# Attention with pooled keys, then a mixture of adapters: the order of operations at the start and at the end of the kernel is written out by hand

## Chip, core and metric

The kernel runs on one core of a Trainium2 chip. The metric is the device time of one execution in microseconds. Engines: PE (TensorE, matmuls and transposes), DVE (VectorE), ACT (ScalarE), POOL (GpSimd), and SP, which only issues DMAs here. Each engine takes its instructions strictly in the order in which they stand in its queue.

## What is computed

`q` is 4 x 12288 x 128, `kv` is 4 x 384 x 32 x 128, all fp32.

```python
kv_pool = kv.reshape(B, H//4, 4, W//4, 4, C).mean(axis=(2, 4))    # 768 keys per batch
k = v = kv_pool.reshape(B, -1, C) @ w_sr
a = softmax(q @ k.T / sqrt(C))
x = (a @ v).reshape(B * N, C)                                     # 49152 rows
logits = x @ w_gate                                               # 8 experts, the best 2 used
delta = sum over the two: softmax weight * (x @ A[e]) @ B[e]      # rank 16
return x + delta
```

## The kernel before

The 49152 rows are cut into 96 chunks of 512 rows, 24 to a batch (`NB = 24`). Four chunks share one load of q (`GC = 4`). Keys come in J = 6 blocks of 128, handled as three pairs r = 0, 1, 2. For a chunk k the steps are the following (line numbers of the kernel before; all matmuls go through line 68):

- `scores(k, r)` (238): two matmuls of 128x512 into an `sg` tile of PSUM (two tiles, `ps_s`), then the exp on ACT into `em` (246).
- `attend(k, s)` for four quarters s (248): six matmuls of 128x137 each from `em` and `vx` into `acc`, of which there is one tile (`ps_a`).
- `normalize(k)` (256): on DVE a reciprocal and a product, from `acc` to `xn`. `xn` holds the 128 outputs and the 8 logits. The next chunk's attend can't write `acc` before it.
- `top(k)` (276): four MAX8 on DVE. `route` (285): comparisons on POOL (for chunks 0 and 1 on DVE). `gates` (310): a tanh on ACT and two products on POOL. Chunks are routed in pairs up to slot 71 and singly in the last batch.
- `transposes(kx, kh, engine)` (319): transposes x of one chunk and hg of an older one on PE into one PSUM tile `tt_ps`, and copies both to SBUF (`tts`) in one copy on DVE or ACT.
- `down(k)` (342), `gate(k)` (347), `up(k)` (356), `finish(k)` (361): x @ A to `h_ps`, times the gate weights on DVE (`hg`), hg @ B to `d_ps`, plus x on DVE (`osb`), and the output DMA from SP.

The PSUM tiles of q's transposes, key preparation, `tt_ps`, `h_ps` and `d_ps` share two banks (`ps_m`, tag `mb`). `osb` has six tiles.

The keys of batch 0 are prepared at the start: kv comes in 24 DMAs of 256 KB (98), DVE adds rows (`pair_step`, 175), PE transposes and sums them to `kpT`, multiplies with w_sr to `kfT` (`keys`, `keys2`) and to `vx` (`values`). For later batches POOL adds (`pool_step`, 163) while the chunks of the batch before run; nine small steps on PE and DVE follow (`rest`). q of groups 0 and 1 is loaded as fp32 and transposed on PE (`turn_q`, 107); later groups are cast to bf16 by a DMA issued from POOL (`cast_q`, 77) and transposed by a DMA from SP (`load_qT`, 82). Before each cast POOL copies one column of the qT of the group before, which makes it wait for that.

The order is that of a Python program with `keep` (program order per engine). A prologue (372 to 400) computes the scores of chunks 0 to 3 while the keys of batch 0 arrive. Then one loop (420 to 498) has a slot for each k from 4 to 95. In the plain slot, k of 9 and more:

```python
scores(k, 0); gates of an older group; normalize(k-2)
transposes(k-6, k-7, DVE); scores(k, 1); up(k-8); finish(k-8)
attend(k-1, 0); top(k-2); route (every other slot); scores(k, 2)
down(k-6); gate(k-6); a step of key preparation; attend(k-1, 1..3)
```

The dictionary `att` puts two attends into slots 6, 7 and 8, and `enter` lets two chunks instead of one enter the adapters in slots 73, 74 and 76, so that in the end the lag from chunk to adapter is shorter; their second transposes are copied by ACT. After the loop a written-out end (503 to 657) handles the adapters of chunks 91 to 95: `carry` copies d_ps to SBUF on ACT, `add_there` adds x on POOL, for two chunks; the last chunk's routing runs on DVE; the last two chunks are handled in halves.

Of the kernel before, what the change touches and what calls it, by code (L numbers as in the profile page):

```python
# [20 lines left out]
def kernel(  # L21
# [85 lines left out]
    def turn_q(g, m, engine):  # L107
        if m == 0:
            qT[g] = qpool.tile([P, GT], BF16, tag="qT", name="qT")
        ps = mtile([P, S, P], name="qT_ps")  # L110
        for i in range(S):
            mm(ps[:, i], q_f[g][:, m * S + i], id_f, is_transpose=True,
               start=(i == 0), stop=(i == S - 1))
        o = qT[g][:, m * T:(m + 1) * T].rearrange("p (s t) -> p s t", s=S)
        if engine is nc.scalar:
            keep(nc.scalar.copy(o, ps))
        else:
            keep(nc.vector.tensor_copy(o, ps))
# [39 lines left out]
    def prepare(b, adder):  # L158
# [28 lines left out]
        def keys(h):  # L187
            if h == 0:
                st["kpT"] = prep.tile([P, J, P], FP32, tag="kpT", name="kpT")
                kfT[b] = per_b.tile([P, J, P], BF16, tag="kfT", name="kfT")  # L190
            kpT = st["kpT"]
            ps = mtile([P, 2, P], name="kpT_ps")
# [4 lines left out]
            for n, (r, i, c) in enumerate(parts):  # L197
                mm(ps[:, i], kvr[b, h][:, r, i, c * C:(c + 1) * C], id_f, is_transpose=True,
                   start=(n == 0), stop=(n == len(parts) - 1))
            keep(nc.vector.tensor_scalar(kpT[:, 2 * h:2 * h + 2], ps, 1.0 / 16.0, None,  # L200
# [27 lines left out]
        for h in range(3):  # L228
            for f in (keys, keys2, values) if adder is nc.vector else (keys, values, turn):
                rest.append(lambda h=h, f=f: f(h))  # L230
# [7 lines left out]
    def scores(k, r):  # L238
        b = k // NB
        if r == 0:  # L240
# [7 lines left out]
    def attend(k, s):  # L248
        b = k // NB
        if s == 0:  # L250
# [5 lines left out]
    def normalize(k):  # L256
        ri = rpool.tile([P, S], FP32, tag="rinv", name="rinv")
        keep(nc.vector.reciprocal(ri, acc[k][:, :, VC]))  # L258
        k0, m = first[k], k - first[k]
        if m == 0:  # L260
            xg[k0] = xpool.tile([P, GC, S, VC], FP32, tag="xn", name="xn")
        x = xg[k0][:, m]
# [13 lines left out]
    def top(k):  # L276
        k0, m = first[k], k - first[k]
        if m == 0:
# [4 lines left out]
    later = []  # L283

    def route(k0):
        n = size[k0] * S
        eng = nc.gpsimd if k0 > 1 else nc.vector
        lg = xg[k0].rearrange("p m s c -> p (m s) c")[:, 0:n, C:VC]
# [72 lines left out]
    def finish(k):  # L361
# [5 lines left out]
        for d in (em, acc, xn, xT, hgT, hp, hg, dp):  # L367
            d.pop(k, None)

    LA = 4  # L370

    for m in range(GC):
        turn_q(0, m, nc.scalar)
    sums, rest = prepare(0, nc.vector)
    for h in range(3):
        for item in sums[h]:
            item()
        rest[3 * h]()
        if h > 0:
            scores(2, h - 1)  # L380
        rest[3 * h + 1]()
        if h > 0:
            scores(3, h - 1)
            rest[3 * h - 1]()
        scores(0, h)
        scores(1, h)
    rest[8]()
    scores(2, 2)
    scores(3, 2)
    rest = []  # L390

    late = const.tile([P, 1], FP32)
    keep(nc.gpsimd.tensor_copy(late, q_f[1][:, GC * S - 1, 0:1]))
    for g in range(2, 4):
        cast_q(g)
    a_bf = const.tile([P, P], BF16)
    keep(nc.vector.tensor_scalar(a_bf, a_f, 0.5, None, op0=ALU.mult))
    b_bf = const.tile([P, C], BF16)
    keep(nc.vector.tensor_copy(b_bf, b_f))
    turn_q(1, 0, nc.scalar)  # L400


    att = {LA: [0], LA + 1: [1], LA + 2: [2, 3], LA + 3: [4, 5], LA + 4: [6, 7]}
    for k in range(8, NCHUNK):
        att[k + 1] = [k]
    normed = {}
    for t, ks in att.items():
        for k in ks:
            normed[k] = t + 1 if k == ks[-1] else t
    ready = {k: normed[first[k] + size[k] - 1] + 1 for k in range(NCHUNK)}  # L410
    enter, t, left = {}, LA, list(range(NCHUNK - 3))
    while left:
        can = [k for k in left if ready[k] <= t]
        enter[t] = can[:2] if t in [NB * (B - 1) + 1 + i for i in (0,1,3)] else can[:1]
        left = [k for k in left if k not in enter[t]]
        t += 1

    sums, rest = [], []
    kh, ku, kd, kdone = [], [], [], []
    for k in range(LA, NCHUNK):  # L420
        b, i = divmod(k, NB)
        ka = att.get(k, [])
        kx = enter.get(k, [])
        if k % GC == 0:
            g = k // GC
            if 2 <= g + 1 < B * NG:
                load_qT(g + 1)
        if b + 1 < B:
            i0 = 4 if b == 0 else 0
            if i == i0:  # L430
                sums, rest = prepare(b + 1, nc.gpsimd)
                sums = sum(sums, [])
            if i0 <= i < i0 + 12:
                h, j = divmod(i - i0, 4)
                load_kv(b + 1, h, j, None)

        if k % GC == 2 and 4 <= k // GC + 2 < B * NG:
            keep(nc.gpsimd.tensor_copy(late, qT[k // GC + 1][:, 0:1]))
            cast_q(k // GC + 2)

        def after_norm(kn):
            top(kn)
            if kn == first[kn] + size[kn] - 1:
                route(first[kn])

        kn = [n for n in att.get(k - 1, []) if normed[n] == k]
        if k == LA:
            for s in range(S):
                attend(0, s)
            ka = []  # L450
        scores(k, 0)
        while later:
            later.pop(0)()
        for x_ in kd:
            down(x_)
        for n in kn:
            normalize(n)
        pairs = [(kx[j] if j < len(kx) else None, kh[j] if j < len(kh) else None)
                 for j in range(max(len(kx), len(kh)))]
        for x_, h_ in pairs[:1]:  # L460
            transposes(x_, h_, nc.vector)
        for x_ in kd:
            gate(x_)
        if k + 1 in range(GC + 1, 2 * GC):
            turn_q(1, (k + 1) % GC, nc.scalar)
        scores(k, 1)
        for u_ in ku:
            up(u_)
            finish(u_)
        for a_ in ka[:-1]:  # L470
            for s in range(S):
                attend(a_, s)
            normalize(a_)
            after_norm(a_)
        if ka and len(ka) == 1:
            attend(ka[0], 0)
        for n in kn:
            after_norm(n)
        scores(k, 2)
        for x_ in kx[:1]:  # L480
            down(x_)
            gate(x_)
        kd = []
        if rest and i in ((14, 15, 16, 18, 19, 20, 21, 22, 23) if b == 0 else (11, 12, 13, 17, 18, 19, 21, 22, 23)):
            rest.pop(0)()
        for a_ in ka[-1:]:
            for s in range(1 if len(ka) == 1 else 0, S):
                if s == S - 1:
                    for x_, h_ in pairs[1:]:
                        transposes(x_, h_, nc.scalar)  # L490
                        kd = [x_] if x_ is not None else []
                attend(a_, s)
        ku = kh
        kh = kx[:1] + kdone
        kdone = kd
        if b + 1 < B and i % 2 == 0 and (8 if b == 0 else 6) <= i <= 20:
            for _ in range(4 if b == 0 and i % 4 else 3):
                sums.pop(0)()
# [189 lines left out]
```

## Time and profile before

| | us |
|---|---|
| median of 3 runs | 400.73 (400.01 to 401.08) |
| the profiled execution, its own time | 401.02 |
| its span, first to last instruction | 399.24 |
| busy: PE, DVE, ACT, POOL | 378.6, 324.4, 297.2, 201.8 |
| first `sg` matmul of slots 0, 14, 72, 95 | 15.22, 75.04, 293.65, 382.99 |

"Busy" is the time in which an instruction of the engine runs. PE's matmuls are pipelined, and the shown length of one contains its way through the array, so a busy PE may still have time to give. An idle time is put down to what ended it ("<-"); the number behind it in the lists of waits is the sum, the count, the longest. The chain is the work that ended last, followed back from the end.

### The profile page before, as it was taken

What the parts mean: (1) busy time and instruction counts of PE and PEld (TensorE: products, weight loads), DVE (VectorE), ACT (ScalarE), POOL (GpSimd) and SP (SyncE); (2) the same over time, 40 slices, a digit from 0 to 9 for tenths busy, and PEclk for the clock granted to TensorE, in tenths of its full rate; (3) what the DMA queues carried; (4) which work ended last, traced back from release to release, by engine and by line L of the source; (5) the groups of instructions that cost most, each with busy time, mean ns of one, the idle gap of its engine ahead of it and who ended that gap; (6) DMA issues with size and microseconds to landing.
All of it is one profiled execution on the core that took longest, in us unless ns stands there. A gap on an engine that the chain in (4) does not pass through costs nothing.

```text
span 399.2 us, 11711 instructions
## 1 busy us (share of the span) xinstructions
PE 378.6 (95%) x4589; PEld 301.6 (76%) x4589; DVE 324.4 (81%) x944; ACT 297.2 (74%) x375; POOL 201.8 (51%) x471
## 2 busy tenths in 40 slices
PE   3798899999999999999999999999999899999994
PEld 2556777788878888888877888888877688788882
DVE  2553678898988888888988888898888788888885
ACT  2379467877877887786877887786878778888873
POOL 0010059988613486877613486877614244344443
PEclk9999999999999999999999999999999999999996
DMA  7999728895679899955669999956754477464113
GB/s 292 361 262 247 176 88 221 245 269 139 155 124 304 259 257 301 238 135 133 159 151 260 281 266 304 219 136 139 153 135 106 133 186 159 135 145 121 64 71 135
DMA packets 71464, 76.47 MB, mean 192 GB/s; under 512 B 49936, under 2 KB 50704, under 8 KB 70928
## 3 DMA queue, kind: packets, MB, share of 16 engines
q1 hardware_dynamic: 70272, 63.98, 54.4%
q0 software_dynamic: 704, 11.54, 16.6%
q8 instruction: 36, 0.59, 0.6%
q10 hardware_dynamic: 432, 0.20, 0.2%
q14 instruction: 20, 0.16, 0.2%
HBM read 50.53 MB, written 36.70 MB: 218 GB/s over the span
## 4 chain that ended last, share of the span: by engine, by line
PE 83%; DVE 4%; POOL 4%; ACT 3%; DMA 3%; SPq 1%; issue 1%; ACTq 0%; DVEq 0%; POOLq 0%
PE acc L68 32%; PE sg L68 28%; PE tt_ps L68 10%; PE d_ps L68 5%; PE h_ps L68 5%; ACT em L246 2%; POOL kvr L171 2%; DMA w_sr_sb<-in_w_sr_dram 1%; PE kpT_ps L68 1%; SPq L98 1%; DMA kvr<-in_kv_dram 1%; PE v_ps L68 1%; DVE xn L263 1%; DVE tts L336 1%; PE kfT_ps L68 1%
## 5 line engine op out<-in xcount | busy, mean ns | idle before, releaser
L246 ACT ACTIVATE em<-sg 128x1024 f16<-128x1024 f32 x288 | 280.5, 1023 | 78.7 <-PE sg L68 78.6
L68 PE MATMUL sg<-qT,kfT 128*128 128x512 bf16 x576 | 171.1, 379 | 3.1 <-ACT em L246 2.6
L68 PE MATMUL acc<-vx,em 128*128 128x137 f16 x2280 | 167.5, 223 | 1.2 <-DVE xn L263 1.2
L68 PEld LDWEIGHTS <-em 128*128 128x128 f16 x2304 | 145.4, 98 | 3.2 <-DVE xn L263 2.2
L68 PEld LDWEIGHTS <-tts 128*128 128x128 bf16 x740 | 56.4, 98 | 46.1 <-issue 2.8
L263 DVE TENSOR_TENSOR xn<-acc,rinv 128x544 f32<-128x544 f32 x95 | 68.8, 724 | 3.4
L293 POOL TENSOR_TENSOR over<-xn,srt 128x64 f32<-128x64 f32 (+1 forms) x116 | 30.3, 282 | 81.0 <-DVE srt L281 81.0
L350 DVE TENSOR_TENSOR hg<-h_ps,gw 128x512 bf16<-128x512 f32 x93 | 64.2, 691 | 7.4 <-PE h_ps L68 0.2
L171 POOL TENSOR_TENSOR kvr<-kvr 128x512 f32<-128x512 f32 x54 | 67.3, 1272 | 0.0
L336 DVE COPY tts<-tt_ps 128x1024 bf16<-128x1024 bf16 (+1 forms) x90 | 61.9, 688 | 1.7 <-PE tt_ps L68 0.9
L363 DVE TENSOR_TENSOR osb<-d_ps,xn 128x512 f32<-128x512 f32 x91 | 62.6, 690 | 0.6 <-PE d_ps L68 0.6
L314 POOL TENSOR_TENSOR gw<-th,over 128x64 f32<-128x64 f32 (+1 forms) x58 | 16.9, 291 | 69.1 <-ACT th L312 69.0
L68 PEld LDWEIGHTS <-kfT 128*128 128x128 bf16 x576 | 45.8, 98 | 6.7 <-issue 4.3
L258 DVE RECIPROCAL rinv<-acc 128x4 f32<-128x4 f32 x95 | 17.3, 182 | 35.5 <-PE acc L68 35.2
L68 PEld LDWEIGHTS <-xn 128*128 128x128 bf16 x384 | 29.1, 98 | 20.9 <-DVE xn L263 0.4
L68 PE MATMUL d_ps<-b_bf,tts 128*128 128x128 bf16 x364 | 35.1, 219 | 1.6 <-DVE tts L336 1.1
L68 PE MATMUL h_ps<-a_bf,tts 128*128 128x128 bf16 x372 | 36.0, 219 | 0.3 <-ACT tts L334 0.3
L68 PE MATMUL tt_ps<-id_bf,xn 128*128 128x128 bf16 x372 | 35.9, 219 | 0.0
L68 PE MATMUL tt_ps<-id_bf,hg 128*128 128x128 bf16 x368 | 35.6, 219 | 0.3 <-DVE hg L350 0.3
L281 DVE MAX8 srt<-xn 128x8 f32<-128x8 f32 x380 | 34.2, 152 | 0.2
L68 PEld LDWEIGHTS <-hg 128*128 128x128 bf16 x384 | 25.7, 98 | 1.4 <-issue 0.6
L299 POOL TENSOR_SCALAR over<-over 128x64 f32<-128x64 f32 (+1 forms) x58 | 19.4, 335 | 5.2
(82 smaller groups left out, 200.7 us busy)
## 6 DMA issues: line engine op xcount, KB each, us to landing
out_dram<-osb SPq DMA_DIRECT2D x94, 256.0 KB, 3.2
kvr<-in_kv_dram SPq DMA_DIRECT2D x36, 512.0 KB, 6.3
qbf<-in_q_dram POOLq DMA_DIRECT2D x22, 512.0 KB, 6.0
kvr<-in_kv_dram SPq DMA_DIRECT2D x24, 256.0 KB, 5.2
qf<-in_q_dram SPq DMA_DIRECT2D x1, 1024.0 KB, 5.3
qf<-in_q_dram SPq DMA_DIRECT2D x4, 256.0 KB, 5.2
out_dram<-osb SPq DMA_DIRECT2D x3, 128.0 KB, 2.2
qT<-qbf SPq DMA_TRANSPOSE x22, 5.2
```

The costliest lines, as they stand in the source:

```text
L68: return keep(nc.tensor.matmul(*a, **k))
L171: keep(adder.tensor_tensor(u[:, lo:hi], u[:, lo:hi], v[:, lo:hi], op=ALU.add))
L246: keep(nc.scalar.activation(em[k][:, 2 * r:2 * r + 2], ps, AF.Exp, bias=0.0, scale=scale))
L258: keep(nc.vector.reciprocal(ri, acc[k][:, :, VC]))
L263: keep(nc.vector.tensor_tensor(x, acc[k][:, :, 0:VC], ri.unsqueeze(2).broadcast_to([P, S, VC]), op=ALU.mult))
L281: keep(nc.vector.max(srt[k0][:, m, s], xn[k][:, s, C:VC]))
L293: keep(eng.tensor_tensor(d, lg, so[:, :, i].unsqueeze(2).broadcast_to([P, n, 8]), op=ALU.subtract))
L299: keep(eng.tensor_scalar(mask, mask, 0.0, None, op0=ALU.is_ge))
L314: keep(eng.tensor_tensor(w[:, 0:n], th, mask, op=ALU.mult))
L336: keep(nc.vector.tensor_copy(sb[:, lo:hi], ps[:, lo:hi]))
L350: keep(nc.vector.tensor_tensor(hg[k].rearrange("p s (e r) -> p (s e) r", e=E), hp[k].rearrange("p s (e r) -> p (s e) r", e=E), gw[k0][:, m ...
L363: keep(nc.vector.tensor_tensor(osb, dp[k], xn[k][:, :, 0:C], op=ALU.add))
```

## The change

The prologue, slots 4 to 13, slots 72 to 95 and the end become two lists of short commands that a small interpreter (`follow`) runs one after the other. Slots 14 to 71 come from a function `slot(k)`, which writes the loop's plain slot above in the same commands. The operations themselves stay, with these differences: `xn` tiles are shared by four chunks (`k // GC`) instead of one group; `keys` can be done in two halves; `gates` is a command of its own instead of an entry of `later`; and the steps of the old end (separate transposes of x and hg, halves, `carry` with `add_there`, routing on DVE) may be used for any chunk of the last batch.

```diff
-        k0, m = first[k], k - first[k]
-        if m == 0:
-            xg[k0] = xpool.tile([P, GC, S, VC], FP32, tag="xn", name="xn")
-        x = xg[k0][:, m]
+        if k // GC not in xg:
+            xg[k // GC] = xpool.tile([P, GC, S, VC], FP32, tag="xn", name="xn")
+        x = xg[k // GC][:, k % GC]
...
+    def follow(order):
+        for item in order.replace("\n", " ").split(";"):
+            what, *at = item.split()
+            sub[what](*[None if x == "-" else int(x) if x.isdigit() else x for x in at])
...
+    follow("""
+ad 0 0; tq 0 0 A; ad 0 1; ad 0 2; cs1; tq 0 1 A; ad 0 3; ky 0 0; tq 0 2 V; ky 0 1; k2 0; ad 1 0; va
+0; sc 0 0; tq 0 3 A; lq 2; sc 2 0; ad 1 1; ad 1 2; ad 1 3; ky 1 0; sc 1 0; ky 1 1; ad 2 0; sc 3 0;
+k2 1; ad 2 1; va 1; sc 3 1; ad 2 2; sc 0 1; ky 2 0; sc 2 1; ad 2 3; kv 1 0 0; ky 2 1; sc 1 1; k2 2;
+tq 1 0 V; sc 0 2; va 2; cab; sc 4 2; tq 1 1 V; at 0 2; kv 1 0 1; sc 1 2; at 0 1; sc 4 0; at 0 0; at
+0 3; sc 2 2; nm 0; tq 1 2 V; sc 5 1; kv 1 0 2; at 1 3; at 1 0; at 1 2; at 1 1; sc 6 2; nm 1; tq 1 3
+V; sc 3 2; at 2 1; tp 1; at 2 3; sc 6 1; tp 0; at 2 2; at 2 0; sc 6 0; nm 2; ro 1; tt 0 - V; tt 1 -
+V; ro 0; tp 2; sc 7 0; ga 1; pa 1 0; at 3 2; at 3 0; sc 4 1; tt 2 - V; sc 5 0; kv 1 0 3; at 3 3; at
+3 1; nm 3; dn 1; ga 0; sc 8 1; dn 0; sc 9 0; lq 3; ge 1; at 4 3; at 4 1; sc 5 2; tp 3; ro 2; at 4 2;
+at 4 0; sc 7 2; ge 0; ga 2; nm 4; tt - 1 A; sc 8 0; tt 3 - V; at 5 2; at 5 1; at 5 3; at 5 0; sc 8
+2; nm 5; dn 2; sc 7 1; tp 4; tt - 0 V; at 6 0; at 6 3; tp 5; at 6 1; ge 2; cq 4; at 6 2; nm 6; up 0;
+sc 10 1; fi 0; sc 9 2; ro 4; up 1; at 7 0; kv 1 1 0; at 7 3; kv 1 1 1; at 7 2; ga 4; ca 1; pd 1; pa
+1 1; at 7 1; nm 7; dn 3; kv 1 1 2; tp 6; sc 9 1; sc 10 2; kv 1 1 3; tt 4 - A; ge 3; at 8 2; at 8 0;
+pa 1 2; at 8 1; at 8 3; sc 11 0; sc 11 2; nm 8; tp 7; dn 4; tt 5 - V; at 9 2; at 9 3; pa 1 3; lq 4;
+sc 10 0; ge 4; kv 1 2 0; ro 6; tt - 2 V; pa 1 4; ga 6; at 9 0; at 9 1; dn 5; nm 9; ge 5; sc 12 1; sc
+12 0; tt - 3 V; tp 8; tp 9; at 10 2; at 10 3; up 2; pa 1 5; tt - 4 V; sc 11 1; at 10 1; at 10 0; fi
+2; nm 10; up 3; tt 6 5 V; fi 3; sc 12 2; sc 13 2; kv 1 2 1; tp 10; at 11 1; dn 6; at 11 0; at 11 2;
+ge 6; up 4; pa 1 6; ca 4; at 11 3; nm 11; sc 13 0; up 5; ro 8; tt 7 - V; sc 13 1; pa 1 7; at 12 1;
+dn 7; fi 5; pd 4; tp 11; ge 7; pa 1 8; at 12 0; at 12 3; ga 8; at 12 2; tt - 6 A; ro 10; pa 1 9
+""")
+    for k in range(14, 72):
+        follow(slot(k))
+    follow("""
+ga 68; sc 72 0; hb 75 mb; sc 73 0; xt 66 mb; db 72 mb; db 66 sg; db 64 mb; nm 70; lq 19; hb 65 mb;
+ht 65 0 4; at 71 2; db 65 sg; db 67 mb; at 71 3; sc 72 2; cx 66 V; dn2 66 mb; sc 72 1; at 71 1; ch
+65 0 4 V; at 71 0; ge2 66 0 2; ge2 66 2 4; sc 73 2; nm 71; tt 67 66 V; hb 77 mb; xt 68 mb; tp 70; sc
+73 1; at 72 1; at 72 0; dn2 67 sg; cx 68 V; up2 64 0 4; at 72 3; ca 64; up2 65 0 4; ge2 67 0 2; ge2
+67 2 4; ca 65; db 69 mb; cq 20; at 72 2; sc 74 0; tp 71; nm 72; ro 70; tt 69 67 V; xt 70 mb; cx 70
+A; sc 74 1; at 73 1; sc 74 2; db 73 mb; ga 70; dn2 68 mb; dn2 69 mb; at 73 0; at 73 3; up2 66 0 2;
+up2 66 2 4; ca 66; ge2 69 0 2; ge2 69 2 4; ge2 68 0 4; at 73 2; sc 75 1; nm 73; tt 71 69 V; up2 67 0
+2; tp 72; up2 67 2 4; pd 64; pd 65; sc 75 0; at 74 0; db 93 sg; hb 68 mb; sc 77 0; ro 72; dn2 70 mb;
+at 74 3; lq 20; af 67 0 4 ACT; ge2 70 0 4; ht 68 0 4; sc 76 0; tp 73; ch 68 0 2 V; ch 68 2 4 V; dn2
+71 mb; at 74 1; at 74 2; db 68 mb; ge2 71 0 4; nm 74; pd 66; sc 75 2; tt 72 71 V; sc 79 0; tt 73 70
+V; db 71 sg; sc 76 1; at 75 3; ga 72; up2 69 0 4; sc 77 1; at 75 0; tp 74; at 75 2; af 69 0 4 SP; ro
+73; up2 68 0 4; dn2 72 mb; db 70 mb; ca 68; ge2 72 0 4; db 74 mb; at 75 1; ga 73; nm 75; sc 76 2; cq
+21; ro 74; dn2 73 mb; tt 74 72 V; sc 78 1; ga 74; at 76 1; at 76 2; dn2 74 mb; up2 71 0 2; up2 71 2
+4; at 76 0; ge2 73 0 4; ca 71; hb 73 mb; sc 77 2; at 76 3; hb 83 mb; lastroute 75; up2 70 0 4; sc 78
+2; ge2 74 0 4; nm 76; tt 75 74 V; lt 75; sc 78 0; tp 76; ro 76; pd 68; af 70 0 4 SP; at 77 1; ga 76;
+at 77 2; at 77 3; lg_ 75; dn2 75 sg; up2 72 0 4; at 77 0; ca 72; ge2 75 0 4; sc 80 0; xt 76 mb; nm
+77; cx 76 V; sc 79 1; db 75 mb; tp 77; ht 75 0 2; ht 75 2 4; at 78 1; ht 73 0 2; ht 73 2 4; ch 75 0
+4 V; sc 81 0; ro 77; ch 73 0 4 V; up2 74 0 4; at 78 3; dn2 76 sg; up2 73 0 4; at 78 0; ca 73; db 81
+mb; ge2 76 0 2; db 77 sg; ge2 76 2 4; ga 77; at 78 2; db 76 mb; ca 74; nm 78; db 78 mb; tp 78; sc 79
+2; sc 80 1; ro 78; hb 80 mb; db 84 mb; lq 21; up2 75 0 4; tt 77 76 V; at 79 0; sc 80 2; at 79 3; dn2
+77 sg; at 79 1; pd 71; hb 78 mb; xt 78 mb; ga 78; at 79 2; ca 75; ge2 77 0 4; sc 81 1; up2 76 0 4;
+cx 78 V; ht 77 0 4; nm 79; sc 81 2; at 80 1; cq 22; ch 77 0 4 V; ca 76; dn2 78 mb; tp 79; ro 79; sc
+82 0; at 80 3; at 80 0; at 80 2; ga 79; xt 79 mb; ge2 78 0 4; nm 80; cx 79 A; ht 78 0 4; hb 81 mb;
+sc 85 0; sc 82 1; lastroute 80; ch 78 0 2 V; at 81 2; dn2 79 mb; pd 74; lq 22; at 81 0; up2 77 0 4;
+at 81 3; ca 77; lt 80; at 81 1; ge2 79 0 4; ch 78 2 4 V; sc 82 2; nm 81; up2 78 0 2; sc 83 1; tt 80
+79 V; hb 86 mb; tp 81; up2 78 2 4; at 82 3; hb 82 mb; af 78 0 4 SP; pd 72; lg_ 80; db 82 mb; sc 83
+0; db 80 mb; at 82 1; dn2 80 mb; sc 83 2; ro 81; at 82 2; ge2 80 0 2; ge2 80 2 4; at 82 0; xt 81 mb;
+ga 81; nm 82; cx 81 A; sc 84 1; ht 80 0 4; sc 84 2; at 83 3; xt 82 mb; ch 80 0 4 V; at 83 1; dn2 81
+mb; sc 84 0; lastroute 82; pd 73; cx 82 V; at 83 0; lt 82; db 79 mb; at 83 2; up2 79 2 4; ge2 81 0
+2; ge2 81 2 4; dn2 82 mb; up2 79 0 2; nm 83; ca 79; sc 85 1; sc 85 2; at 84 0; cq 23; lg_ 82; ge2 82
+0 4; tp 83; up2 80 0 2; up2 80 2 4; ro 83; at 84 3; at 84 1; at 84 2; sc 86 2; sc 86 0; ht 81 0 4;
+db 91 sg; fi 80; ga 83; nm 84; hb 84 mb; xt 83 mb; at 85 1; tp 84; at 85 0; sc 87 1; ch 81 0 4 V; ht
+82 0 2; ht 82 2 4; db 83 mb; pd 76; lq 23; cx 83 V; sc 86 1; at 85 3; ch 82 0 2 V; ch 82 2 4 V; dn2
+83 mb; ro 84; ge2 83 0 4; up2 81 0 4; ca 81; at 85 2; sc 87 0; xt 84 mb; ga 84; db 85 mb; sc 89 0;
+ht 83 0 2; ht 83 2 4; hb 95 sg; nm 85; tp 85; at 86 2; hb 93 mb; cx 84 V; at 86 3; ro 85; sc 87 2;
+at 86 0; ch 83 0 2 V; ch 83 2 4 V; pd 77; ga 85; dn2 84 mb; db 89 mb; ge2 84 0 4; up2 82 0 2; up2 82
+2 4; ca 82; at 86 1; sc 88 2; nm 86; xt 85 mb; sc 88 0; up2 83 0 2; up2 83 2 4; at 87 0; cx 85 V; ht
+84 0 4; ch 84 0 2 V; db 86 sg; af 83 0 4 SP; sc 89 1; hb 90 mb; at 87 2; sc 88 1; tp 86; at 87 1; ro
+86; dn2 85 mb; ch 84 2 4 V; ga 86; sc 92 0; at 87 3; up2 84 0 2; up2 84 2 4; ge2 85 0 2; sc 94 0;
+ge2 85 2 4; nm 87; tp 87; tt 86 85 V; db 87 mb; sc 89 2; at 88 3; at 88 0; pd 82; sc 92 2; af 84 0 4
+SP; up2 85 0 4; ca 85; hb 87 mb; dn2 86 sg; ro 87; at 88 2; ge2 86 0 4; at 88 1; nm 88; db 90 mb; xt
+87 mb; cx 87 A; sc 90 2; ga 87; hb 94 acc; ht 86 0 4; sc 90 1; at 89 1; ch 86 0 4 V; lastroute 88;
+xt 88 mb; dn2 87 mb; ge2 87 0 2; ge2 87 2 4; at 89 3; sc 90 0; lt 88; at 89 2; cx 88 V; at 89 0; nm
+89; ht 87 0 2; ht 87 2 4; sc 91 0; sc 91 1; ch 87 0 4 V; hb 92 acc; tp 89; ro 89; dn2 88 mb; at 90
+2; at 90 0; up2 86 2 4; lg_ 88; at 90 3; up2 86 0 2; ca 86; ge2 88 0 4; at 90 1; ga 89; sc 91 2; up2
+87 0 4; nm 90; tt 89 88 V; sc 92 1; at 91 3; pd 81; tp 90; ro 90; at 91 2; pd 85; dn2 89 sg; at 91
+1; ga 90; af 87 0 4 ACT; db 88 mb; at 91 0; ge2 89 0 4; sc 93 0; nm 91; tt 90 89 V; sc 93 1; at 92
+1; at 92 3; up2 88 0 4; dn2 90 mb; sc 93 2; at 92 2; pd 75; lastroute 91; lt 91; ge2 90 0 4; db 94
+mb; at 92 0; sc 95 0; xt 91 mb; af 88 0 4 SP; sc 94 1; up2 89 0 4; nm 92; at 93 0; cx 91 V; lg_ 91;
+ht 90 0 4; pd 79; af 89 0 4 SP; db 92 acc; dn2 91 sg; ge2 91 0 2; o95 95; at 93 2; ge2 91 2 4; at 93
+3; tp 92; ch 90 0 4 A; sc 94 2; at 93 1; ro 92; up2 90 0 4; nm 93; db 95 sg; ga 92; sc 95 1; tt 92
+91 V; sc 95 2; tp 93; at 94 1; at 94 0; xt 93 sg; dn2 92 mb; cx 93 A; at 94 3; af 90 0 4 SP; at 94
+2; pt 95 0 4; dn2 93 mb; ge2 92 0 4; nm 94; pt 95 4 6; up2 91 0 2; up2 91 2 4; ht 92 0 4; xt 94 mb;
+ro 93; ga 93; tp 94; ge2 93 0 2; nm 95; ca 91; pd 86; cx 94 A; xt 95 sg; ht 93 0 2; ch 92 0 4 V; ro
+94; pd 91; ga 94; lastroute 95; cx 95; up2 92 0 4; lt 95; dn2 95 sg; ge2 93 2 4; ht 93 2 4; ca 92;
+lg_ 95; pd 92; dn2 94 mb; ge2 95 0 4; ge2 94 0 4; ch 93 0 4 A; ht 95 0 4; ch 95 0 2 A; up2 93 0 4;
+ch 95 2 4 V; ht 94 0 2; ht 94 2 4; af 93 0 4 SP; ch 94 0 2 A; ch 94 2 4 A; up2 95 0 4; up2 94 0 4;
+af 95 0 4 ACT; af 94 0 2 ACT; af 94 2 4 SP
+""")
```

The commands: `tq` turn_q, `ad` pair_step, `ky`, `k2`, `va` keys, keys2, values of batch 0, `cab` the casts of A and B, `cs1` the first two q casts, `cq` a later one, `lq` load_qT, `kv` load_kv, `pa` one POOL add of the next batch's kv, `pr` one step of `rest`, `sc` scores, `at` attend, `nm` normalize, `tp` top, `ro` route, `ga` gates, `tt` transposes, `dn` down, `ge` gate, `up` up, `fi` finish. For the last batch: `xt` transposes x alone, `cx` copies it (A is ACT, V is DVE), `ht` and `ch` the same for hg, `dn2`, `ge2`, `up2` are down, gate, up with a chosen PSUM tile or in parts lo to hi of the four quarters, `af` is the add on DVE with its DMA, `ca` with `pd` are carry and add_there, `lastroute`, `lt`, `lg_` the routing of one chunk on DVE with its tanh and its weights, `pt` attend over a part of the keys for all quarters. `hb` and `db` name the PSUM tile that a later `ht` or `up2` writes: `mb`, `sg` or `acc`. In the last list there are 13 `tt`, 17 `xt`, 25 `ht`, 30 `dn2`, 18 `ca` with `pd` and 14 `af`.

## The prediction

> **What bounds the kernel now.** I read the page first, then busy time by stretch, then the chain, the waits and the timeline at both ends.
>
> ```profile
> span 399.2 us, 11711 instructions
> PE 378.6 (95%) x4589; PEld 301.6 (76%) x4589; DVE 324.4 (81%) x944; ACT 297.2 (74%) x375; POOL 201.8 (51%) x471
> PEclk9999999999999999999999999999999999999996
> ```
>
> PE is nearly always busy and its clock is full until the last slice. Busy time cut at the slots where the lists begin and end (slot k starts with the first `sg` matmul of chunk k; columns: window, its length, busy PE, PEld, DVE, ACT, POOL, clock, DMA share, GB/s):
>
> ```profile
> 7.60:26.99 19.39, 16.91 (x96) 11.60 (x96) 10.94 (x21) 9.45 (x12) 1.28 (x3) 1.00 0.97 343
> 26.99:75.04 48.05, 44.14 (x518) 34.24 (x516) 31.64 (x110) 35.70 (x45) 20.51 (x39) 1.00 0.71 178
> 75.04:293.65 218.61, 218.61 (x2744) 177.13 (x2741) 194.17 (x561) 169.68 (x203) 137.21 (x268) 1.00 0.82 210
> 293.65:324.43 30.78, 29.01 (x370) 22.73 (x368) 25.12 (x68) 24.20 (x32) 11.06 (x42) 1.00 0.56 141
> 324.43:386.62 62.19, 62.06 (x790) 49.89 (x788) 54.32 (x154) 51.04 (x69) 26.37 (x106) 1.00 0.45 122
> 386.62:399.24 12.62, 7.02 (x87) 5.34 (x84) 7.52 (x26) 5.64 (x14) 4.68 (x11) 0.76 0.32 116
> ```
>
> Slots 14 to 71 leave PE no gap. There, in the records, a matmul starts 216 ns (`sg`), 60 (`acc`) or 56 (128 columns) after the one before. A plain slot is 6 x 216 + 24 x 60 + 16 x 56 = 3632 ns, and the chain returns each 3.63 us:
>
> ```profile
> 331.27 1.08 PE acc L68 x18
> 334.90 1.08 PE acc L68 x18
> 338.53 1.08 PE acc L68 x18
> ```
>
> So these intervals are a floor, and I price both ends with them: `sc` 0.432 us, one `at` 0.36, any four 128-column matmuls 0.224, an fp32 `tq` 0.42, `va` 0.46. "Busy" overstates: two `sg` matmuls before a stall are shown as 0.59.
>
> **Head.** After 26.99 us (first score on the last third of the keys) PE has 34 `sc` (14.69), 52 `at` (18.72), 29 adapter steps (6.50), four `tq` (1.68) and one `va` (0.46): 42.1 us. It takes 48.05. The waits in that window name the lost 6.0:
>
> ```profile
> ACT th L312 <- POOL over L298: 5.2, 3, 3.3
> DVE gw L314 <- ACT th L312: 4.1, 1, 4.1
> PE sg L68 <- ACT em L246: 2.4, 6, 0.8
> PEld L68 <- DVE xn L263: 2.2, 4, 0.6
> ```
>
> These are fixed orders that meet too early: an attend behind the normalize that must free the single `acc` tile, a tanh in front of exps.
>
> **Tail.** From slot 72 on there are 72 `sc` (31.1), 100 `at` (36.0) and 123 adapter steps (27.6): 94.7 us, to 388.3 by the floor, but the last matmul starts at 395.4. Slots 74 to 79, where chunks enter two at a time, lose 3.2 us (4.65, 4.70, 4.58, 5.51, 3.85, 4.14 against 4.08, 4.08, 4.30, 4.08, 3.86, 3.86 for the matmuls they hold); the drain loses the rest. Three lines of the timeline:
>
> ```profile
> 303.24 0.38 PE L68 MATMUL d_ps<-b_bf,tts 128*128 128x128 bf16 x4 [0.35 <-DVE tts L336]
> 315.97 0.40 PE L68 MATMUL h_ps<-a_bf,tts 128*128 128x128 bf16 x4 [0.31 <-ACT tts L334]
> 395.76 0.42 DVE L558 TENSOR_TENSOR osb<-tail_ps,xn 128x256 f32<-128x256 f32 x1 [0.46 <-PE tail_ps L68]
> ```
>
> **The change, part by part.** The middle is emitted in the order of before, so at its floor: 0.
>
> *Up to the last third of the keys.* The last piece of kv is issued at 17.9 us and lands 5.2 later, at 23.1; no order changes that. Before, its adds ran 21.84 to 24.33, behind a `vx` copy, and the score came at 26.99. The list puts two of the four adds ahead (their pieces land at 19.9 and 20.5), so the last ends at 23.1 + 0.69 = 23.8; from last add to a ready kfT the trace needs 2.4: score at 26.2. Gain 0.8, and one `tq` (0.42) moves into that shadow.
>
> *26.2 to slot 14.* PE then has 41.6 us. I walked the list with durations of the trace: exp 0.93 in a run, normalize 1.1 from last attend to usable `xn`, tts copy 0.41 (one half) or 0.69, hg and osb 0.69, routing of one chunk on DVE 0.85. Every `nm` now has 1.3 us of other matmuls ahead of the next `at` (such as `sc 2 2; tq 1 2; sc 5 1`). The 15 exps from `sc 0 2` to `sc 9 0` end at 41.0 while PE is at 41.5: ACT just keeps up. One stall appears: `nm 3` stands behind `ro 1`, two tts, `ro 0`, `ga 1`, `tp 2` and one more tts on DVE, ends near 42.0, and costs 0.55 before `at 4 3`; small ones 0.3. `sc 8 1` at 40.4 needs qT of group 2, which landed at 31.35 + 4.5 = 35.9. Slot 14 at 68.6. For waits that a hand walk misses I add 0.5: **69.1, gain 5.9**.
>
> *POOL in the head.* From about 52 us it has, before slot 14, nine kv adds (8 x 1.27 + 0.73), two output adds (2 x 1.27), three routings (1.42 each) and two gates (0.72): 19 us in 17. Behind a late routing stands a tanh, behind that the exps. By the walk `ro 10` has its argument at 69.6, after the exp of `sc 14 0` would be under way, so nothing is lost there, but POOL enters slot 14 about 1.9 us later than before; its tanh two slots on may wait 0.6, once: **+0.3** (0 to 1.5).
>
> *Tail, 24 slots.* PE work is the same 94.7. DVE: 26 normalizes at 0.88, 20 `tp`, 6 `lastroute` at 0.95 and `lg_` 0.19, 13 paired copies 0.66, 10 `cx` and 20 `ch`, gates 0.65 (halves 0.36), 14 adds: 85 us. ACT: 72 exps at 0.93, 18 carries and 10 copies near 0.5, 26 tanhs at 0.12: 84. POOL: 53. Everything but PE has some 10 us to spare, and between any two normalizes only one stretch gives ACT more than PE (4.77 to 4.72). I walked the first 10 us: no bubble. PE work up to the last attend is 91.7, so it ends at 385.4 at the floor; with 0.8 for bubbles 386.2 (before 388.98). Then `nm 95` takes 1.1 and DVE's remaining queue 5.5 (before 7.2 in all), then from add to end 3.06 as before (396.18 to 399.24): 395.9. **Gain 3.4** (1.5 to 4.2).
>
> *The 20 carries with output adds on POOL, against a rule.* Two output adds of 1.27 us run on POOL now; the lists make 20. The Trainium skill, "SBUF — State Buffer", section "SBUF: two separate sides", says VectorE and GpSimd take one port pair as an exclusive lock, and a DVE operation with two SBUF inputs waits out a GpSimd one. In the trace hg and osb, with one input in PSUM, take 0.69 with a POOL add beside them and without (31 and 62, 21 and 70 instances), so for these I take 0. The operations of `lastroute` and `lg_` do read two SBUF tensors; in the trace `both` took 0.274 beside a POOL add, the larger `arg` and `mk` 0.20 and 0.18 after it. By the rule 6 x 4 such operations could wait up to 1.27 each, 30 us of DVE; by the row 0.1 each, 2.4, within DVE's spare 10. I take the row.
>
> *Output tiles.* `pd 75` and `pd 79` come 35 us after their carries, so 4 of the 6 osb tiles serve the rest; with 3.2 us to landing each request finds one free, twice with under 0.5 us margin. Bounds 0 to 1; it is in the 0.8.
>
> Sum: span 399.2 - 5.9 + 0.3 - 3.4 = 390.2. The profiled execution took 401.02, 1.8 around its span, 0.3 over the median 400.73; taken from the median: **391.7**.
>
> **Rivals.** (a) Likeliest, as summed: 391.7, own range 389.5 to 394.3; 0.62.
>
> (b) One end pays half or less: POOL's backlog passes to ACT through the tanhs (head gain 3 instead of 5.9), or the drain keeps its length and slots lose 2 us (tail gain 0.5). Either way near 395; 0.25. For it: ACT already waits 5.2 us for POOL in the head. Against: by the walk it has the argument in time.
>
> (c) The lists do not change what PE meets, because data and banks, not order, set the ends: 399.5 to 401.9; 0.05. Against: the gaps are waits behind an instruction that could stand elsewhere.
>
> (d) Slower, by the two `mb` banks of PSUM in the tail. Copies of x and hg, so far one tile per chunk, are often split: some 89 tiles instead of three per slot, so a bank has 2 x 94.7 / 89 = 2.1 us per tile instead of 2.42. Tiles live 1.1 to 1.4 us now. If DVE, 90% full, fetches them late, the next tile's first matmul holds PE. The 9 us of gain are gone from a wait of 0.10 us per tile; at 0.15 the kernel takes 405. Against: PE waits for no bank from 328 to 386 now, and 7 `dn2` and several others use `sg` banks. 0.08.
>
> **How the numbers follow.** Within 0.3% (399.5 to 401.9, about what a measurement of this kernel can tell from no change) lies (c): 0.05. Slower is (d), 0.08. Faster 0.87. The range 388.8 to 398.0 takes in the bounds of (a) and (b).
>
> **What would show it.** Right: slot 14 near 69, slot 72 still 218.6 to 219 later, the last attend about 92.5 us after slot 72, PE without gaps of over 0.3 in slots 74 to 79, DVE the drain's engine. Wrong: ACT's `th` waiting for POOL before slot 18; PE's d_ps, h_ps or tail tiles waiting for DVE or ACT copies all over the tail; `sc 92 0` waiting for its qT, for which the cast (5.8) and transpose (5.2) behind `cq 23` leave 2 us; each gap there is lost one for one.

## The result, and the profile after

| | before | after |
|---|---|---|
| median, us | 400.62 (400.01 to 401.08) | **394.28** (394.03 to 394.60) |
| the profiled execution / its span | 401.02 / 399.24 | 394.46 / 392.59 |
| slot 14 starts | 75.04 | 67.69 |
| slot 14 to slot 72 | 218.61 | 218.66 |
| slot 72 to the end of the span | 105.59 | 106.24 |

The ratio is 0.9843 [0.9826, 0.9860]: 6.3 us faster, where 9.0 were forecast (391.7 from 400.73). The head gave 7.36 us (forecast 5.9), the middle nothing (forecast -0.3), and the tail, for which a gain of 3.4 was forecast, lost 0.65. One execution of all those below, of the kernel with one meeting moved, took 1774 us, with the matmuls of the scores at 1382 ns instead of 379, and its ratio leaves it out.

First two lines from the page of the changed kernel, then its busy time by stretch (window, length, busy PE, PEld, DVE, ACT, POOL, clock, DMA share, GB/s), cut at the first score on the last third of the keys, slots 14 and 72, and in the tail.

```profile
span 392.6 us, 11742 instructions
PE 375.7 (96%) x4589; PEld 302.2 (77%) x4589; DVE 323.3 (82%) x980; ACT 305.6 (78%) x389; POOL 217.0 (55%) x459
```

```profile
26.03:67.69 41.66, 41.66 (x513) 33.80 (x514) 30.79 (x115) 35.88 (x44) 21.70 (x38) 1.00 0.93 222
67.69:286.35 218.66, 218.66 (x2744) 177.10 (x2742) 194.40 (x561) 170.36 (x204) 140.13 (x273) 1.00 0.81 207
286.35:316.53 30.18, 30.12 (x389) 24.16 (x387) 24.53 (x82) 27.66 (x38) 15.13 (x42) 1.00 0.51 119
316.53:350.00 33.47, 32.31 (x410) 25.78 (x408) 26.66 (x89) 30.80 (x46) 18.02 (x51) 1.00 0.61 145
350.00:380.00 30.00, 28.41 (x365) 22.86 (x363) 25.73 (x83) 25.89 (x36) 15.37 (x42) 1.00 0.29 105
380.00:392.60 12.60, 6.02 (x83) 4.69 (x80) 8.39 (x27) 4.13 (x11) 5.73 (x12) 0.96 0.39 147
```

In the head PE is busy for all of 41.66 us. In the first 30 us of the tail it is busy too: the slots where chunks used to enter in pairs lose nothing now. The losses are new, and lie where before lost nothing: 1.16 us between 316 and 350, 1.59 between 350 and 380. Measured from start to start of the matmuls, PE loses 1.24 us at 330.84, 1.34 at 372.80 and 0.57 at 374.25. What stands around the first two, in the timeline of after:

```profile
327.34 2.50 POOL L468 TENSOR_TENSOR osb<-osb,xn 128x512 f32<-128x512 f32 x2
327.56 1.07 DVE L478 TENSOR_TENSOR both<-so 128x4 f32<-128x4 f32 x1
328.66 1.22 DVE L480 SCALAR_TENSOR_TENSOR arg<-xn,both 128x32 f32<-128x32 f32 x1
329.81 0.18 DVE L483 TENSOR_TENSOR mk<-xn,so 128x32 f32<-128x32 f32 x1
330.84 0.27 PE L68 MATMUL tail_ps<-b_bf,tt 128*128 128x128 bf16 x2 [1.08 <-DVE hg L439]
...
369.60 2.50 POOL L468 TENSOR_TENSOR osb<-osb,xn 128x512 f32<-128x512 f32 x2
369.70 1.22 DVE L480 SCALAR_TENSOR_TENSOR arg<-xn,both 128x32 f32<-128x32 f32 x1
370.84 1.30 DVE L483 TENSOR_TENSOR mk<-xn,so 128x32 f32<-128x32 f32 x1
372.80 0.38 PE L68 MATMUL tail_ps<-id_bf,xn 128*128 128x128 bf16 x4 [1.18 <-DVE hg L439]
```

The same three small operations of a `lastroute` take 1.07, 1.22 and 0.18 us in chunk 80 and 0.18, 1.22 and 1.30 in chunk 91. Of these, each that starts while a POOL output add runs is long, and it ends 0.02 to 0.05 us after an add ends: 327.34 + 1.27 = 328.61 and 328.63, then 329.84 and 329.88. (`mk` of chunk 80 starts only 0.03 us before its add ends.) Chunk 82 (`both` 0.79) and chunk 95 (0.90) show it too; chunks 75 and 88, with no add near, take 0.16 to 0.20 everywhere. Added over the list, VectorE loses 5.4 us.

**Theory** ("port lock" in the expectations): the adds on POOL hold the port pair that the prediction tells of, VectorE's operations with two SBUF inputs wait until an add ends, and PE waits for VectorE. **Rivals**: VectorE is simply too full in the tail; or PE's waits for the two `mb` banks, the prediction's case (d), are the cause and the long operations only stand nearby.

### The profile page after: what moved, and what is told of

It is laid out like the page before. It is cut to its first block, busy times and chain, and to the rows that moved or that the text cites. A ratio compares the mean times of both kernels' runs of the same rounds, so it can differ in the third digit from the quotient of the medians.

```text
span 392.6 us, 11742 instructions
## 1 busy us (share of the span) xinstructions
PE 375.7 (96%) x4589; PEld 302.2 (77%) x4589; DVE 323.3 (82%) x980; ACT 305.6 (78%) x389; POOL 217.0 (55%) x459
## 4 chain that ended last, share of the span: by engine, by line
PE 86%; DVE 5%; DMA 3%; SPq 1%; POOL 1%; ACT 1%; issue 1%; DVEq 0%; ACTq 0%; POOLq 0%
PE acc L68 33%; PE sg L68 31%; PE tt_ps L68 9%; PE h_ps L68 4%; PE d_ps L68 4%; PE tail_ps L68 3%; SPq L98 1%; DMA w_sr_sb<-in_w_sr_dram 1%; DMA kvr<-in_kv_dram 1%; PE v_ps L68 1%; PE kpT_ps L68 1%; DVE hg L439 1%; ACT em L252 1%; DVE osb L457 1%; PE kfT_ps L68 1%
## 5 line engine op out<-in xcount | busy, mean ns | idle before, releaser
L68 PE MATMUL acc<-vx,em 128*128 128x137 f16 x2280 | 170.1, 223 | 0.4 <-DVE xn L268 0.4
L68 PEld LDWEIGHTS <-tts 128*128 128x128 bf16 x628 | 46.9, 98 | 30.0
L335 DVE COPY tts<-tt_ps 128x1024 bf16<-128x1024 bf16 (+1 forms) x82 | 53.9, 658 | 2.0 <-PE tt_ps L68 1.8
L349 DVE TENSOR_TENSOR hg<-h_ps,gw 128x512 bf16<-128x512 f32 x66 | 45.5, 690 | 4.7 <-PE h_ps L68 0.2
L362 DVE TENSOR_TENSOR osb<-d_ps,xn 128x512 f32<-128x512 f32 x62 | 42.8, 691 | 0.0
L68 PE MATMUL tt_ps<-id_bf,xn 128*128 128x128 bf16 x316 | 30.4, 219 | 0.1
L68 PE MATMUL tt_ps<-id_bf,hg 128*128 128x128 bf16 x312 | 30.1, 219 | 0.0
L468 POOL TENSOR_TENSOR osb<-osb,xn 128x512 f32<-128x512 f32 x20 | 25.3, 1270 | 0.5 <-ACT osb L464 0.5
L68 PE MATMUL h_ps<-a_bf,tts 128*128 128x128 bf16 x264 | 25.5, 219 | 0.0
L68 PE MATMUL d_ps<-b_bf,tts 128*128 128x128 bf16 x256 | 24.7, 219 | 0.0
```

What stands on the lines that cost most here:

```text
L68: return keep(nc.tensor.matmul(*a, **k))
L335: keep(nc.vector.tensor_copy(sb[:, lo:hi], ps[:, lo:hi]))
L349: keep(nc.vector.tensor_tensor(hg[k].rearrange("p s (e r) -> p (s e) r", e=E), hp[k].rearrange("p s (e r) -> p (s e) r", e=E), gw[k0][:, m ...
L362: keep(nc.vector.tensor_tensor(osb, dp[k], xn[k][:, :, 0:C], op=ALU.add))
L468: keep(nc.gpsimd.tensor_tensor(dp[k], dp[k], xn[k][:, :, 0:C], op=ALU.add))
```

## The experiments

**Which end pays what.** Two kernels with half of the change each: the list of the head with the old slots 72 to 95 and end, and the old start with the list of the tail.

> The list for the preparation and the first ten slots with slots 72 to 95 and the end as they were before. By the traces the head alone is worth 7.3 us and the old tail is 0.7 us shorter than the new: 400.6 - 7.3 = 393.3 us (392.8 to 393.8), so faster than the changed kernel. If instead the tail's list did pay and the head's gain only looks so large because the cut at slot 14 flatters it, this run is over 394.3 us, up to 396.

> The preparation and the first ten slots as before, with the list for slots 72 to 95 and the end. By the traces the tail's list alone gives nothing: 400.6 + 0.7 = 401.3 us (400.8 to 401.8). If the tail's list pays what was forecast, 397.2 us; if the two lists only pay together, well over 402.

Measured: 393.63 us, ratio 0.9830 [0.9817, 0.9843], and 401.56 us, ratio 1.0019 [1.0012, 1.0027]. The head's list is worth 7.0 us, the tail's list alone costs 0.9, and the two add up: -6.1 against -6.3. The second kernel's trace again has `both` and `arg` of chunk 80 at 1.07 and 1.22 us.

That trace is of an execution of 400.23 us, one of three near 400.3 among the 17; the others took 401.28 to 402.05. In it `mk` of chunk 91 is short, and the gap of 1.34 us behind it is missing:

```profile
377.64 1.33 POOL L468 TENSOR_TENSOR osb<-osb,xn 128x512 f32<-128x512 f32 x1
377.65 0.18 DVE L483 TENSOR_TENSOR mk<-xn,so 128x32 f32<-128x32 f32 x1
```

In the changed kernel the same pair stands the same way, the add at 370.829 and `mk` at 370.843, 0.014 us apart in both traces. There `mk` waited and the add took 1.27; here `mk` went through and the add took 1.33. The starts that the trace shows do not tell which of the two will wait. That the other fourteen executions lost this draw fits their 1.3 us, but no trace of one was kept.

**The lock, with PE's order untouched.** POOL's output adds moved in the list:

```diff
-... lastroute 80 ...; pd 74; ...; pd 72; ... lastroute 82; pd 73; ... pd 81; ... pd 85; ... pd 75; lastroute 91; ... pd 79
+ro 77; pd 72   ro 79; pd 74   ro 81; pd 73   cq 23; pd 75   ro 83; pd 79   ro 87; pd 81   ro 89; pd 85
```

> The changed kernel with seven of its GpSimd output adds (pd 72, 73, 74, 75, 79, 81, 85) moved in the list so that none should run while VectorE does both, arg and mk of a lastroute; the order of every other operation on TensorE, ScalarE and VectorE is that of the changed kernel. Port-lock theory: both, arg and mk of chunks 80, 82 and 91 fall from 0.8-1.3 us to about 0.2 us each, TensorE's idle times of 1.24, 1.34 and 0.57 us in the tail go, and the time falls by about 3 us to 391.3 us. Rival (the tail's shortfall comes from VectorE simply being full, or from the waits for two banks): these three operations aren't the cause, the gaps stay or move by under 0.3 us each, and the time stays at 394.3, give or take 0.4.

Measured: 392.07 us, ratio 0.9785 [0.9772, 0.9798]; 2.2 us faster than the changed kernel, not 3. The operations of chunks 80, 82 and 91 fall to 0.17 to 0.19 us and the three gaps go. But PE has two new ones, 0.99 us at 328.49 and 0.33 at 329.41. The timeline of this kernel, first the operations of chunk 80, then what stands before the new gap:

```profile
327.42 0.17 DVE L478 TENSOR_TENSOR both<-so 128x4 f32<-128x4 f32 x1
327.62 0.19 DVE L480 SCALAR_TENSOR_TENSOR arg<-xn,both 128x32 f32<-128x32 f32 x1
327.73 0.18 DVE L483 TENSOR_TENSOR mk<-xn,so 128x32 f32<-128x32 f32 x1
...
326.06 0.18 POOL L512 CAST late<-qT 128x1 f32<-128x1 bf16 x1 [2.94 <-DMA qT<-qbf]
327.73 0.23 ACT L311 ACTIVATE th<-over 128x32 f32<-128x32 f32 x1 [1.33 <-POOL over L304]
328.49 0.40 PE L68 MATMUL tail_ps<-a_bf,tt 128*128 128x128 bf16 x4 [0.83 <-ACT tt L396]
```

The second part is read from the bottom: PE waits for a copy on ACT, which stands behind a tanh, which waits for POOL's routing, which stands behind `cq 22`, which waits for the transposing DMA `lq 21`. That left SP at 319.28 instead of 316.96, because the output of `pd 72` now stands ahead of it in SP's queue and waits for its add.

**One meeting alone.** The changed kernel with only `pd 75` and `pd 79` moved, the two at chunk 91; a second, single execution gives the profile.

> The changed kernel with only pd 75 and pd 79 moved, the two adds that ran beside arg and mk of chunk 91. Port-lock theory: the two gaps of TensorE behind that lastroute (1.34 and 0.57 us) go and the one of 1.24 us behind chunk 80 stays: 394.3 - 1.9 = 392.4 us (392.0 to 392.8). Rival (VectorE is full, and what is taken from one place shows up at the next): 393.5 or more.

> The changed kernel with only pd 75 and pd 79 moved, once more for its profile (its time is from the run before). Port-lock theory: arg and mk of chunk 91 take about 0.2 us each and TensorE's gaps of 1.34 and 0.57 us are gone; both and arg of chunk 80 still take 1.07 and 1.22 us and the gap of 1.24 us behind them is still there. Time about 392.3 us.

Measured: 392.27 us, ratio 0.9793 [0.9780, 0.9806], so 2.0 us for one meeting; the profiled execution took 392.97. In its trace chunk 91 has 0.17, 0.19 and 0.18 us and no gap behind it, while at chunk 80 `both` and `arg` take 1.08 and 1.22 and the gap stays: it shows as 1.46, but one `sg` matmul just ahead of it is missing from this trace, which is worth 0.22, so it is 1.24 as before. What is taken from one place does not come back at the next, as it would if VectorE were full.

**Routing left on POOL.** `lastroute`, `lt`, `lg_` of chunks 75, 80, 82, 88, 91 replaced by `tp`, `ro` and `ga`.

> The changed kernel with the lastroute of chunks 75, 80, 82, 88 and 91 replaced by the ordinary route (its tests, four of them on GpSimd) at the same places; only chunk 95 keeps its own. VectorE loses 15 small operations, which cost about 2.7 us if nothing hinders them and about 8 us as the trace of after shows them. Port-lock theory: same as with the moved adds, about 391.3 us (390.5 to 392.5), unless GpSimd's later gates make TensorE wait. Rival (fullness of VectorE): a gain of well under 1 us, since 2.7 us of a queue that was not full is not seen: 393.7 or more. The form in which VectorE is full throughout can't be told from the lock by this run alone.

Measured: 392.85 us, ratio 0.9809 [0.9795, 0.9823]: 1.4 us faster than the changed kernel. Only chunk 95 has a long operation left. One gap of 0.96 us (PE behind an `osb` on VectorE, 333.88) is new and was not followed further. The gain lies between what the lock theory (3) and the fullness rival (under 1) said, so this run decides little; the one before it and the next one do.

**The lock by itself.** Series of single operations, no data between them.

> Nothing of the reference is computed here: zeros are written out, and VectorE and GpSimd run short series of single operations on tiles of their own, with no dependency inside a series. VectorE: scalar_tensor_tensor 128x32 and tensor_tensor 128x512 (two SBUF inputs), tensor_tensor 128x512 with one input in PSUM, max of eight, a copy of 128x512 out of PSUM and one from SBUF to SBUF; first each beside an idle GpSimd, then each beside eight GpSimd adds of 128x512. Last, scalar_tensor_tensor beside GpSimd adds of 128x32, fills and copies of 128x512, and tensor_tensor 128x512 beside fills. Port-lock theory: beside the adds the operations with two SBUF inputs take up to 1.3 us each, one per add (about 1.25 us from start to start, against 0.1 to 0.2 alone); those with an input in PSUM and max keep their times; the copy from SBUF to SBUF[...] is open. Beside fills, which read no SBUF, no wait. Rival (the long operations in the tail waited for a semaphore or for something of their own chunk): scalar_tensor_tensor stays at about 0.2 us beside the adds.

The timeline of that program (start, length of the series, operation, count). The first three series run beside an idle POOL:

```profile
7.84 2.67 DVE L84 SCALAR_TENSOR_TENSOR vo<-va,vb 128x32 f32<-128x32 f32 x12
10.92 4.31 DVE L86 TENSOR_TENSOR vo<-va,vb 128x512 f32<-128x512 f32 x6
31.61 3.65 DVE L90 COPY vo<-va 128x512 f32<-128x512 f32 x8
...
47.33 7.40 DVE L84 SCALAR_TENSOR_TENSOR vo<-va,vb 128x32 f32<-128x32 f32 x12
59.20 9.16 DVE L86 TENSOR_TENSOR vo<-va,vb 128x512 f32<-128x512 f32 x6
72.83 5.76 DVE L87 TENSOR_TENSOR vo<-pp,vb 128x512 f32<-128x512 f32 x8
84.44 3.22 DVE L88 MAX8 v<-va 128x8 f32<-128x8 f32 x16
107.63 10.37 DVE L90 COPY vo<-va 128x512 f32<-128x512 f32 x8
119.78 2.80 DVE L84 SCALAR_TENSOR_TENSOR vo<-va,vb 128x32 f32<-128x32 f32 x12
126.10 2.67 DVE L84 SCALAR_TENSOR_TENSOR vo<-va,vb 128x32 f32<-128x32 f32 x12
131.64 6.09 DVE L84 SCALAR_TENSOR_TENSOR vo<-va,vb 128x32 f32<-128x32 f32 x12
```

Beside adds of 128x512, 12 of the small operations take 7.40 us instead of 2.67: five of them 1.13 to 1.15 us, and between these one goes through at 0.19. Not one wait per operation, then, but two operations per add. The 128x512 with two SBUF inputs goes from 0.69 to 1.63 us each, and stretches POOL's adds in turn, from 1.26 to 1.59. With one input in PSUM (`pp`) it stays at 0.69, MAX8 at 0.17. The copy from SBUF to SBUF waits as well: 0.43 to 1.37. Beside POOL adds of 128x32 (119.78), about 0.25 us each, the series of small operations takes 2.80 instead of 2.67. Beside fills of POOL (126.10) nothing waits; beside its copies (131.64) an operation takes 0.64. The rival's 0.2 us beside the adds is excluded.

**The queue of SP.** `lq 21` put ahead of `pd 72`:

```diff
-ro 77; pd 72; ...; lq 21
+ro 77; lq 21; pd 72; ...
```

> The kernel with the seven moved adds, with one more item moved: lq 21, the issue of a transposing DMA, now stands ahead of pd 72. In the run before this one SP held lq 21 behind the output of pd 72, which waits for that add (issue at 319.3 us, 317.0 in the changed kernel); GpSimd's cq 22 then waited 2.9 us for the transfer, ScalarE's tanh 1.3 for GpSimd, TensorE 0.99 and 0.33 for ScalarE. If that chain is the rest of the tail's shortfall: TensorE's two gaps go, 392.1 - 1.3 = 390.8 us (390.4 to 391.2). Rival (the lock is settled, but VectorE is still what TensorE waits for there): 391.8 or more.

Measured: 392.22 us, ratio 0.9788 [0.9775, 0.9802]: no gain. The chain was right, since `lq 21` leaves at 317.06, `cq 22` no longer holds the routing, and both gaps are gone. But now PE loses 0.63 and 0.56 us at 337.6 and 338.3, behind another meeting in this kernel's timeline, columns as above:

```profile
335.15 1.73 DVE L478 TENSOR_TENSOR both<-so 128x4 f32<-128x4 f32 x1
```

and on POOL, in the same stretch:

```profile
334.95 0.59 POOL L79 DMA_DIRECT2D qbf<-in_q_dram  x1
335.57 1.28 POOL L468 TENSOR_TENSOR osb<-osb,xn 128x512 f32<-128x512 f32 x1
```

POOL, no longer held up, reached `cq 23` and `pd 75` while VectorE did chunk 82. `both` spans the rest of the cast's issue and the whole add, and ends at 336.88, 0.03 after it.

**Third order.** On top of it `pd 75` goes behind `pd 79`, after `ro 83`.

> The kernel with the moved adds and lq 21 ahead of pd 72, with pd 75 put behind pd 79, after ro 83. In the run without this, the freed GpSimd reached the issue of cq 23's cast and pd 75 early enough to meet both of chunk 82, which took 1.73 us, 335.15 to 336.87, through the rest of the issue (0.39) and the whole add (1.27); TensorE lost 0.63 and 0.56 behind it. Port-lock theory: both of chunk 82 takes at most 0.6 us (the issue may still hold it up), the two gaps go, and the time is 392.2 - 1.2 = 391.0 us (390.6 to 391.5). If the tail gives back whatever is freed, because some other wait is next within a few tenths everywhere: 392.0 or more.

Measured: **390.86 us**, ratio 0.9754 [0.9741, 0.9768], 3.4 us faster than the changed kernel; every operation on PE, ACT and VectorE stands in the changed kernel's order. No long operation is left except `both` of chunk 95, and between 316 and 378 us, from start to start of the matmuls, no gap over 0.23 us (one missing record looks like 0.22, and 74 of 4589 are missing in this trace).

**The drain, twice.** First, as a variant of the kernel with `lq 21` moved: `pd 86` behind `ro 92`, the last projection of chunk 91 ahead of `pt 95`, `pd 91` ahead of `ro 94`. Then, on top of the third order, only `pd 91` behind `pd 92`.

> As the kernel with the moved adds and lq 21, and in the drain pd 86 behind ro 92, the last projection of chunk 91 (up2 and its copy) ahead of pt 95, and pd 91 ahead of ro 94, so that no add runs beside the lastroute of chunk 95, whose both took 0.90 us of which some 0.7 are the wait. Port-lock theory: both falls to about 0.2, and as the drain hangs on VectorE the time falls by 0.3 to 0.7 more, to about 390.3 us. Rival (the drain is bound by the chain of the last chunk through TensorE and ScalarE): both falls, the time stays at that of the kernel without this, within 0.2.

> The kernel with the third order, with one item moved: pd 91 behind pd 92, so that GpSimd has no add to run while VectorE does the lastroute of chunk 95, and every other engine's order stays. Port-lock theory with a drain that hangs on VectorE: both of chunk 95 falls from 0.90 to about 0.2 us, hg of chunk 93, on which TensorE waits 0.68 us right after it, comes 0.7 earlier, and the time falls from 390.9 to about 390.2 us (390.0 to 390.5). Rival (the drain is set by the chain of the last chunk through TensorE and ScalarE, as the earlier trial at the drain suggested, which changed the order on TensorE too): both falls, the time stays within 0.2 of 390.9.

Measured: 392.21 us, ratio 0.9784 [0.9763, 0.9805] (392.22 without), and 391.11 us, ratio 0.9762 [0.9749, 0.9776] (390.86 without). `both` falls to 0.17 and 0.25 us, and no time is won (the executions of the first spread from 390.62 to 393.12, so a few tenths would not show there). In the second the last VectorE add ends 0.76 us earlier (384.69, was 385.45), yet the span ends at 389.0 as before. The DMA issues of the last 9 us, with KB and us from issue to landing, in the third order:

```profile
out_dram<-osb ACTq DMA_DIRECT2D x1, 256.0 KB, 2.1
out_dram<-osb SPq DMA_DIRECT2D x1, 128.0 KB, 2.3
```

and with `pd 91` moved:

```profile
out_dram<-osb ACTq DMA_DIRECT2D x1, 256.0 KB, 2.8
out_dram<-osb SPq DMA_DIRECT2D x1, 128.0 KB, 3.0
```

The output of chunk 91, which used to leave early (380.79), now leaves after that of chunk 92, at 383.56, within 1.2 us of the last four. The last three of these are issued 0.76 us earlier and take 0.73 to 0.78 us longer to land; the very last lands at 387.76, against 387.79. DMA runs at 372 to 410 GB/s for 2.3 us without a break there, in the third order at 372 to 416 for 1.6. So the rival was right that the time stays, though by these landings for another reason than it gave: what VectorE won went to the wait for the DMAs. Whether an order exists that frees `both` and still sends chunk 91 early was not tried.

## Why the prediction was right in kind and short in size

| from the profiles, us | before | forecast | after | third order |
|---|---|---|---|---|
| start to slot 14 | 75.04 | 69.1 | 67.69 | 67.59 |
| slot 14 to 72 | 218.61 | 218.9 | 218.66 | 218.61 |
| slot 72 to the last `xn` | 96.47 | 93.7 | 96.46 | 93.05 |
| last `xn` to the last VectorE add | 6.07 | 5.5 | 6.21 | 6.20 |
| last add to the end | 3.05 | 3.06 | 3.57 | 3.57 |

The one meeting in the kernel before from which the prediction took its price, in the timeline of before:

```profile
389.55 1.27 POOL L567 TENSOR_TENSOR osb<-osb,xn 128x512 f32<-128x512 f32 x1
390.57 0.27 DVE L606 TENSOR_TENSOR both<-so 128x4 f32<-128x4 f32 x1
```

- **The first score on the last third of the keys** was forecast at 26.2 and came at 26.03.
- **The head's walk** had the right PE sum (41.6, measured 41.66) and waits that did not come: the stall of 0.55 behind `nm 3`, 0.3 of small ones, 0.5 for what a walk misses. VectorE reached `nm 3` at 40.05 and had `xn` at 40.99, not near 42.0; `at 4 3` followed without a wait. This is the 1.4 us that the head gave beyond the forecast.
- **POOL's backlog**, +0.3, did not show: slot 14 to 72 is 0.05 longer, and in it PE waits for nothing.
- **Slots 74 to 79** are clean, as forecast: 30.12 of 30.18 us busy.
- **"I take the row"** is the step that failed, and the largest mis-sized term: 0.1 us per operation, and nothing for PE. The 0.274 us `both` of before started 0.25 us ahead of the end of its add (390.57, add until 390.82), so the row showed the tail of a wait, not its length. In the changed kernel those that start within 0.22 us of an add's start take 1.07 to 1.30 us. The Trainium skill ("SBUF — State Buffer", "SBUF: two separate sides") says that a VectorE operation with two SBUF inputs and a GpSimd one that reads SBUF exclude each other for the whole instruction, and the trace agrees: 5.4 us of VectorE lost in 6 operations. The prediction's 24 possible meetings at 1.27 (30 us) were far too many, as only 6 of the 24 were held up. And "within DVE's spare 10" was an average; the spare does not lie where the wait does. PE lost 3.4 us before the last `xn`: 96.46 against 93.05 with only POOL's and SP's queues reordered. Forecast there was 93.7, with 0.8 for bubbles, of which the third order shows next to nothing.
- **The drain** was forecast as VectorE's queue of 5.5 and 3.06 to the end, and took 6.21 and 3.57. Of the first, 0.6 is `both` of chunk 95: without that meeting the queue is 5.61 (379.08 to 384.69). Of the second, 0.4 is the last transfer: it takes 2.31 us from issue to landing instead of 1.90, with two others issued only 0.23 and 0.66 us ahead of it (before: 0.89 and 1.08).
- **Rivals.** (b) allowed for a weak tail, by waits over the slots: near 395, where 394.28 was measured, but the cause was not named. Of (d) a piece came true: PE's tail tiles did wait for VectorE's fetches, but at a few places and by 1.2 us, not by 0.1 at each tile; with the adds moved and the banks as they are, these waits go, so two banks are enough for this list.

The sum, from forecast to result: -1.4 (head), -0.25 (middle), +2.8 (slot 72 to last `xn`), +0.7 (VectorE's drain), +0.5 (to the end) = +2.4 on 391.7, so 394.1; measured 394.28. That the total came as near as it did is in part luck: the tail by itself, forecast at a gain of 1.5 to 4.2, lost 0.65, and the head's 1.4 us beyond the forecast made up a part of it. What the prediction had right is the head, the middle and the work on PE; with POOL's and SP's queues reordered the tail gains 2.8 us (102.8 from slot 72 to the end, against 105.6).

## What to carry to other kernels

A row in which two engines meet can show only the tail of a wait: before you take a price from it, see where in the other engine's instruction it starts. Small operations with two SBUF inputs on VectorE and long adds on POOL are worth a look at each pair that meets, and moving POOL's operation costs no other engine's order, but its DMA moves on SP's queue with it, and whatever it frees arrives early somewhere else. Judge such a move by the trace that comes after it, not by the meeting it removes.

## What the runs showed of the hardware that was not expected

- With POOL's adds back to back, VectorE gets two short operations through per add, one waiting 1.14 us and one not (0.19), at 1.40 us per add; POOL's adds are hardly slowed (1.26 to 1.32).
- An fp32 copy of 128x512 from SBUF to SBUF, which has one input, waits like the operations with two: 0.43 to 1.37 us. So does an operation beside a POOL copy (0.64), not beside a POOL fill (0.19).
- `both` waited through the issue of POOL's cast as well as the add behind it (1.73 us in one run, `mk` 1.74 in the drain's first trial). These two start 0.20 and 0.21 us into the issue; operations of a `lastroute` that start at most 0.14 us into one take 0.18 to 0.19 and do not wait, in six traces. No run takes the issue alone.
- Whether VectorE or POOL goes first is not told by the starts in the trace: with the add 0.014 us ahead of `mk`, `mk` took 1.30 us in one trace and 0.18 in another.
